# Causal attention scores: split products with mask matmuls, replaced by plain fp32 products with the mask on VectorE

## The chip, the core and the metric

The kernel runs on one core of a Trainium2 chip. The metric is the device time of one execution in microseconds (us). The core's engines work side by side, each through a queue of its own that it takes in order: TensorE (PE, with its weight loads as PEld), VectorE (DVE), ScalarE (ACT), GpSimd (POOL) and SyncE (SP), which issues the DMA transfers. They wait for one another by semaphores.

## The reference

Two batches of 448 tokens go through causal attention with 12 heads of 64 channels, then a token mixer and channel mixer, then a Fourier mixer and a second channel mixer. The change touches the attention scores alone:

```python
scale = 1.0 / np.sqrt(q.shape[-1])                     # 1/8
scores = scale * np.matmul(q, k.transpose(0, 1, 3, 2))
mask = np.triu(np.ones((seq, seq), dtype=bool), k=1)
scores = np.where(mask, -1000000000.0, scores)
scores = scores - np.max(scores, axis=-1, keepdims=True)
attn = np.exp(scores)
attn = attn / (np.sum(attn, axis=-1, keepdims=True) + 1e-09)
return np.matmul(attn, v).astype(np.float32)
```

All inputs and outputs are fp32 or, for the weights, fp64 that the kernel converts.

## The kernel before

**The twelve pairs.** Attention runs over 12 pairs of heads (n = 0 to 11, six for each batch). A pair's q and k lie with their 64 channels on partitions 0 to 63 for the first head (e = 0) and 64 to 127 for the second. The 448 query rows are cut into four blocks of 112 (i = 0 to 3); block i needs only the first 112 x (i + 1) keys. A pair passes through these steps, named by one letter each:

- K: DMA of k and q, issued by SP (`load_k`). Before, the targets are idle tiles of the residual (`stage`): a ring of six and, from pair 5 on, of three.
- k, l, q, m (pairs 3 to 11): k and q are split into a high part in fp32r (ACT: `k_high`, and `q_high`, which also scales by 1/8) and a low remainder (POOL: `k_low`; DVE: `q_low`). e (pairs 0 to 2): DVE scales q in place, in two halves.
- S: scores on PE, in groups g. Pair 0 has four groups, one block each; the others three, of which g = 0 holds blocks 0 and 1. Each group takes two neighbouring banks of PSUM, one for each head (`grab` with n=2). Pairs 0 to 2 use plain fp32 matmuls, which PE runs as two passes; pairs 3 to 11 use three fp32r matmuls, high x high, high x low and low x high. Behind them come four bf16 matmuls for a group, which add -1e9 above the diagonal (`maskb`, with `identb` as weights).
- N: DVE takes the negated maximum of a block, both heads in one reduction. E: ACT takes the exponential from PSUM, one instruction for each head, with the negated maximum as bias and the row sum as a second output. The banks are given back after E.
- T: transposes of the exponentials on PE; C: copies of them out of PSUM on DVE and ACT; P: the product with v on PE; O: its copy on ACT; X: transposes back; Z and x: the division by the sums on DVE; h and g: the split of the result on ACT and POOL.

**What sets the order.** The table `ORDER` (line 73) lists these steps, and those of the token mixer that follow each half batch (A, B, D and their copies r, s, b, d, u, w) and of the first weights' conversion (R, W), as one sequence. Every engine takes its own instructions in exactly that sequence. PSUM has eight banks; a step that needs one takes the bank that was given back longest ago, with a preference of pairs for the lower four. Behind the table come the matmuls of the two channel mixers, over weights that ACT and DVE convert from fp64 a few tiles ahead.

**Lines.** The scores are line 366, the mask matmuls 380, the reduction 388, the exponential 398; q scaling 338, q low 342, k low 329, k high 325, q high 334; transposes 412, their copies 421, the product with v 430, the divisors 443 and 444, the division 463.

Of the kernel before, what the change touches and what calls it, by code (L numbers as in the profile page):

```python
# [72 lines left out]
ORDER = """K0 e0.0 S0.1 S0.0 e0.1 K1 S0.2 e1.0 N0.1 K2 N0.0 S0.3 E0.1 N0.2 S1.0 e2.1 E0.0 e1.1 S1.1 N0.3 V0 K3 N1.1 E0.2  # L73
e2.0 N1.0 E0.3 S1.2 T0.2 N1.2 E1.1 V1 C0.2 K4 N1.3 T0.4 T0.0 E1.0 R0 T0.1 T0.3 E1.2 C0.0 S2.1 C0.1 C0.4 S2.0
C0.3 S2.2 E1.3 q3 k3 P0 N2.2 Z0 N2.0 l3 T1.1 N2.1 E2.2 E2.1 O0 m3 T1.2 Z1 T1.0 T1.4 E2.0 N2.3 C1.2 C1.0 E2.3
C1.4 V3 k4 X0 T1.3 x0 S3.0 S3.1 C1.1 l4 Z2 N3.1 q4 S3.2 W0.0 C1.3 N3.0 K5 P1 E3.0 N3.2 T2.0 m4 E3.2 O1 E3.1 T2.2
W0.1 C2.0 T2.1 T2.3 X1 T2.4 B0.0 C2.1 C2.2 N3.3 C2.3 k5 S4.1 b0.0 x1 S4.2 h0 C2.4 E3.3 V2 N4.2 S4.0 P2 T3.2 E4.2
T3.4 N4.3 N4.1 T3.0 l5 W0.2 N4.0 E4.3 R1 g0 K6 W0.3 q5 O2 V5 T3.3 E4.1 X2 T3.1 C3.0 E4.0 C3.4 m5 x2 T4.2 k6 C3.1
T4.0 S5.1 C3.3 C3.2 h2 N5.2 l6 P3 W0.4 E5.2 S5.0 O3 N5.0 C4.0 C4.2 S5.2 g2 B0.2 h1 T4.4 W1.0 T4.3 W0.5 N5.1 N5.3
b0.2 T4.1 C4.1 g1 K7 A0.0 B0.1 C4.4 W1.1 q6 A0.1 R2 q7 V4 m7 C4.3 Z4 E5.0 E5.3 W1.2 E5.1 m6 Z3 r0.0 b0.1 X3 r0.1  # L80
P4 S6.0 O4 S6.1 W1.3 s0.0 W1.4 x3 T5.3 Z5 T5.2 N6.1 T5.1 s0.1 k7 N6.0 C5.3 W1.5 T5.4 C5.2 T5.0 E6.0 C5.1 l7 E6.1
X4 N6.2 C5.0 D0.1 K8 x4 V6 S6.2 E6.2 R3 S7.0 C5.4 W2.0 N6.3 k8 N7.1 S7.1 h4 P5 E6.3 N7.2 V7 D0.0 B1.1 E7.2 q8
T6.4 l8 K9 d0.1 E7.1 O5 T6.0 W2.1 b1.1 g4 X5 m8 T6.2 D0.2 N7.0 C6.0 C6.4 E7.0 x5 d0.0 W3.0 T6.3 T6.1 h5 C6.3
d0.2 C6.2 S7.2 S8.0 S8.1 g5 N7.3 C6.1 h3 N8.0 N8.2 S8.2 k9 N8.1 E7.3 N8.3 g3 P6 T7.3 Z7 E8.2 l9 E8.3 W3.1 q9
T7.0 W2.2 B1.0 C7.3 K10 q10 u0.2 C7.0 W2.3 T7.2 A1.1 Z6 W3.2 T7.4 T7.1 O6 E8.1 A1.0 b1.0 W2.4 B1.2 C7.1 m10 C7.2
C7.4 X6 k10 r1.0 m9 P7 r1.1 s1.0 S9.2 E8.0 b1.2 S9.0 R4 s1.1 O7 x6 S9.1 u0.0 N9.3 h6 T8.4 X7 N9.2 E9.3 N9.1 V8
D1.0 E9.2 x7 V9 C8.4 T8.3 T8.0 T8.2 d1.0 C8.2 N9.0 l10 C8.0 W3.3 K11 g6 T8.1 u1.0 C8.1 w0.2 C8.3 q11 S10.0 u0.1
w1.0 S10.2 E9.1 N10.1 N10.3 P8 k11 N10.0 E9.0 T9.4 T9.2 W3.4 D1.1 m11 Z8 C9.2 O8 E10.3 T9.0 V11 w0.0 E10.1 T9.3
E10.0 l11 D1.2 X8 h7 T9.1 C9.3 d1.1 C9.4 C9.0 d1.2 S11.2 S11.0 W2.5 x8 u1.1 h8 S10.1 N11.3 C9.1 S11.1 N11.0
E11.3 g7 N10.2 E10.2 P9 T10.1 N11.2 T10.0 N11.1 T10.3 E11.0 V10 E11.1 E11.2 C10.3 C10.0 g8 T10.2 Z9 T10.4 w1.1  # L90
C10.4 R5 Z10 A2.0 C10.2 C10.1 P10 W3.5 T11.4 w0.1 O9 T11.2 W4.0 W4.1 T11.0 T11.1 C11.4 O10 u1.2 W5.0 T11.3 W4.2
C11.3 C11.0 C11.1 A2.1 r2.0 C11.2 P11 X9 B2.1 X10 w1.2 W5.1 W4.3 B2.0 r2.1 B2.2 s2.0 s2.1 b2.1 D2.0 x9 R6 W4.4
x10 W5.2 D2.1 W5.3 O11 W4.5 W5.4 Z11 U2 y2 h10 X11 h9 D2.2 z2 b2.0 d2.1 R7 g10 W5.5 x11 d2.0 U0 W6.0 h11 W6.1
B3.0 g11 b3.0 g9 U3 A3.0 y0 y3 A3.1 r3.0 B3.2 b3.2 W6.2 z0 r3.1 s3.0 W7.0 W6.3 s3.1 U1 u2.0 W6.4 D3.1 b2.2 B3.1
D3.0 b3.1 y1 W7.1 W7.2 D3.2 W7.3 u2.1 W6.5 w2.0 W7.4 z1 z3 W7.5 d3.1 d2.2 d3.0 u3.1 w3.1 d3.2 Y0 u2.2 Y1 u3.2
w2.1 u3.0 a0 w3.0 w2.2 a1 w3.2
# [8 lines left out]
def fused_kernel(ctx: ExitStack, tc: tile.TileContext, qk, v, w1, w2, wa, wb, wc, wd, fa, fb, out):  # L105
# [100 lines left out]
    def grab(key, uses=1, n=1):  # L206
        old = {b: i + FAR * ((b < 4) == (n == 2)) for i, b in enumerate(ring)}
        if n == 2:
            old = {b: max(old[b], old[b + 1]) for b in range(0, 8, 2) if b in old and b + 1 in old}
        b = min(old, key=old.get)  # L210
        k = list(range(b, b + n))
        for b in k:
            ring.remove(b)
# [62 lines left out]
    with ExitStack() as actx:  # L276
# [3 lines left out]
        identb = a1.tile([128, 2, TS], BF16, name="identb")  # L280
        maskb = a1.tile([128, 2, 2, TS], BF16, name="maskb")
        vec.memset(identb, 0.0)
        vec.memset(maskb, 0.0)
        for e in range(2):
            for hb in range(2):
                he = slice(D * e, D * e + TS // 2)
                pool.affine_select(
                    out=identb[he, hb], in_=identb[he, hb], pattern=[[-1, TS]], compare_op=ALU.not_equal, fill=1.0,
                    base=hb * TS // 2, channel_multiplier=1,
                )  # L290
                pool.affine_select(
                    out=maskb[he, hb], in_=maskb[he, hb], pattern=[[0, 2], [-1, TS]], compare_op=ALU.is_ge, fill=-1.0e9,
                    base=hb * TS // 2, channel_multiplier=1,
                )
# [9 lines left out]
        staged = [0]  # L304

        def stage(n):
            staged[0] += 1
            return resid[staged[0] % 6 if n < 5 else 3 + staged[0] % 3][1]

        def load_k(n):  # L310
            c = pairs[n]
            b, hp = n // 6, n % 6
# [4 lines left out]
            parts = (slice(0, 2 * TS), slice(2 * TS, S)) if n == 0 else (slice(0, S),)
            for cols in parts:
                for t, part in todo:
                    nc.sync.dma_start(out=t[:, cols], in_=qk[b, hp, :, part, cols])  # L320

        def k_high(n):
            c = pairs[n]
            c.kh, c.kl = [kq.tile([128, S], F32R, tag=t, name=t) for t in ("kh", "kl")]
            act.copy(c.kh, c.k32)

        def k_low(n):
            c = pairs[n]
            (pool if n else vec).tensor_tensor(out=c.kl, in0=c.k32, in1=f(c.kh), op=ALU.subtract)

        def q_high(n):
            c = pairs[n]
            c.qh, c.ql = [kq.tile([128, S], F32R, tag=t, name=t) for t in ("qh", "ql")]
            act.activation(out=c.qh, in_=c.q32, func=AF.Copy, scale=0.125)

        def q_scale(n, part):
            cols = pairs[n].q32[:, 2 * TS * part : 2 * TS * (part + 1)]
            vec.tensor_scalar(out=cols, in0=cols, scalar1=0.125, scalar2=None, op0=ALU.mult)

        def q_low(n):  # L340
            c = pairs[n]
            vec.scalar_tensor_tensor(out=c.ql, in0=c.q32, scalar=0.125, in1=f(c.qh), op0=ALU.mult, op1=ALU.subtract)
# [9 lines left out]

        def scores(n, g):
            c = pairs[n]
            if not hasattr(c, "sp"):
                c.sp, c.se = {}, {}
            sp = c.sp[g] = grab(("S", n, g), 1 if g or not n else 2, 2)
            se = c.se[g] = [sp[:TS, e] for e in range(2)]
            blocks = BLOCKS[g] if n else BLOCKS_0[g]
            for i, c0 in blocks:  # L360
                w = TS * (i + 1) if n < PLAIN else max(256, TS * (i + 1))
                passes = ((c.q32, c.k32),) if n < PLAIN else ((c.qh, c.kh), (c.qh, c.kl), (c.ql, c.kh))
                for m, (qt, kt) in enumerate(passes):
                    for e in range(2):
                        he = slice(D * e, D * e + D)
                        mm(  # L366
                            se[e][:, c0 : c0 + w], lhsT=qt[he, i * TS : (i + 1) * TS], rhs=kt[he, :w],
                            start=m == 0 and (i != 1 or n == 0), stop=False, skip_group_check=True,
                        )
# [674 lines left out]
```

## Time and profile before

| | before |
|---|---|
| median of 3 runs | 682.4 us (682.19 to 682.69) |
| profiled execution, its own time | 681.78 us |
| its span, first to last instruction | 679.9 us |
| PE busy | 674.3 us (99%) |
| DVE busy | 540.2 us (79%) |
| ACT busy | 288.3 us (42%) |
| POOL busy | 124.4 us (18%) |
| PE's share of the chain of work that ended last | 98% |
| granted TensorE clock | 1.000 |

Busy time is the share of the span in which an engine had an instruction under way. The ends of matmuls are modelled, so a full PE row says that PE always had something in it, and not that it went at its peak. An instruction that waits inside the engine, behind another engine's hold of a port, counts as busy. The clock of 1.000 is the higher of TensorE's two levels, 2.4 GHz. The pairs' work lies in the first 102 us or so; the profile's rows for DVE, ACT and POOL are full there and thin out later.

### The profile page before, as it was taken

How to read it: one execution, taken by the hardware profiler on the slowest of the kernel's cores; microseconds unless marked ns; L12 is line 12 of the kernel's file. 1: busy time of each engine (PE TensorE's matmuls, PEld its weight loads, DVE VectorE, ACT ScalarE, POOL GpSimd, SP SyncE). 2: the span in 40 equal slices, each digit the busy share in tenths (PEclk: the TensorE clock that was granted, in tenths of full speed). 3: DMA queues.
4: the chain of work that ended last, by engine and by line, in shares of the span. 5: the costliest groups of instructions: out<-in, count | busy, mean ns of one | idle time of the engine just before them, and what ended most of it. 6: DMA issues, size and time to landing. Idle time of an engine off the chain costs nothing.

```text
span 679.9 us, 10227 instructions
## 1 busy us (share of the span) xinstructions
PE 674.3 (99%) x3922; PEld 618.5 (91%) x3922; DVE 540.2 (79%) x888; ACT 288.3 (42%) x619; POOL 124.4 (18%) x102
## 2 busy tenths in 40 slices
PE   8999999999999999999999999999999999999997
PEld 6888888999999999999999999999999999999997
DVE  6988896597987965799989868989877899646851
ACT  6989894444243332235555522313423333323200
POOL 2235272330000000220330006281002320000000
PEclk9999999999999999999999999999999999999999
DMA  7433311174443332200223332323332533222311
GB/s 213 146 110 130 115 38 70 57 244 143 152 146 117 127 107 93 94 1 1 93 94 104 132 137 94 115 90 136 125 103 83 184 113 138 94 92 76 113 44 55
DMA packets 20865, 73.38 MB, mean 108 GB/s; under 512 B 2366, under 2 KB 7230, under 8 KB 20448
## 3 DMA queue, kind: packets, MB, share of 16 engines
...
q14 instruction: 18, 0.15, 0.1%
...
## 4 chain that ended last, share of the span: by engine, by line
PE 98%; DMA 0%; DVE 0%; SPq 0%; issue 0%; ACT 0%; DVEq 0%
PE psum L242 13%; PE psum L262 13%; PE psum L266 13%; PE psum L267 13%; PE psum L243 13%; PE psum L241 13%; PE psum L430 4%; PE psum L412 4%; PE psum L366 3%; PE psum L499 3%; PE psum L533 2%; PE psum L735 2%; PE psum L804 1%; PE psum L450 1%; PE psum L519 1%; PE psum L380 1%
## 5 line engine op out<-in xcount | busy, mean ns | idle before, releaser
L262 PE MATMUL psum<-gh,wh 128*128 128x448 f32 x432 | 157.5, 365 | 0.0
L242 PE MATMUL psum<-acth,wl 128*128 128x448 f32 x432 | 156.7, 363 | 0.0
L267 PE MATMUL psum<-gl,wh 128*128 128x448 f32 x432 | 156.6, 362 | 0.0
L266 PE MATMUL psum<-gh,wl 128*128 128x448 f32 x432 | 156.6, 362 | 0.0
L241 PE MATMUL psum<-acth,wh 128*128 128x448 f32 x432 | 156.6, 362 | 0.0
L243 PE MATMUL psum<-actl,wh 128*128 128x448 f32 x432 | 156.0, 361 | 0.0
L143 ACT ACTIVATE m<-w 128x512 f32<-128x512 f32 (+2 forms) x92 | 71.1, 774 | 120.2 <-DVE wl L163 83.1
L161 ACT CAST wh<-m 128x512 fp32r<-128x512 f32 (+1 forms) x90 | 63.5, 705 | 94.8 <-PE psum L267 55.5
L241 PEld LDWEIGHTS psum<-acth,wh 128*128 128x128 f32 x432 | 81.0, 188 | 6.1
L267 PEld LDWEIGHTS psum<-gl,wh 128*128 128x128 f32 x432 | 81.0, 188 | 5.9
L262 PEld LDWEIGHTS psum<-gh,wh 128*128 128x128 f32 x432 | 81.1, 188 | 5.7 <-issue 0.2
L266 PEld LDWEIGHTS psum<-gh,wl 128*128 128x128 f32 x432 | 81.0, 188 | 5.7 <-issue 0.2
L242 PEld LDWEIGHTS psum<-acth,wl 128*128 128x128 f32 x432 | 81.1, 188 | 4.9
L243 PEld LDWEIGHTS psum<-actl,wh 128*128 128x128 f32 x432 | 80.9, 187 | 5.2
L150 DVE SCALAR_TENSOR_TENSOR m<-w,m 128x512 uint32<-128x512 uint32 (+2 forms) x92 | 80.3, 873 | 2.3
L163 DVE TENSOR_TENSOR wl<-m,wh 128x512 fp32r<-128x512 f32 (+1 forms) x84 | 69.5, 830 | 14.6 <-ACT wh L161 14.1
L154 DVE SCALAR_TENSOR_TENSOR m<-w,m 128x512 uint32<-128x512 uint32 (+2 forms) x92 | 79.2, 861 | 2.0
L145 DVE TENSOR_SCALAR m<-m 128x512 f32<-128x512 f32 (+2 forms) x92 | 51.2, 557 | 32.1 <-ACT m L143 32.0
L247 ACT ACTIVATE gh<-psum 128x448 fp32r<-128x448 f32 x72 | 37.8, 541 | 69.5 <-PE psum L243 69.3
L249 DVE SCALAR_TENSOR_TENSOR gl<-psum,gh 128x448 fp32r<-128x448 f32 x72 | 43.7, 619 | 29.7 <-ACT gh L247 29.7
L146 DVE TENSOR_SCALAR m<-m 128x512 uint32<-128x512 uint32 (+2 forms) x92 | 49.0, 532 | 2.4
L398 ACT ACTIVATE p<-psum,nmx 112x224 f32<-112x224 f32 (+3 forms) x96 | 46.7, 520 | 6.1 <-DVE nmx L388 5.8
...
## 6 DMA issues: line engine op xcount, KB each, us to landing
...
```

Of the source, the lines that this page charges most:

```text
L143: act.activation(out=m, in_=hi.bitcast(F32), func=AF.Abs)
L145: vec.tensor_scalar(out=m, in0=m, scalar1=F64_MIN, scalar2=F64_MAX, op0=ALU.max, op1=ALU.min)
L150: vec.scalar_tensor_tensor(out=mu, in0=lo, scalar=29, in1=mu, op0=ALU.logical_shift_right, op1=ALU.bitwise_or)
L154: vec.scalar_tensor_tensor(out=mu, in0=hi, scalar=0xC0000000, in1=mu, op0=ALU.bitwise_and, op1=ALU.bitwise_or)
L161: act.copy(wh, m)
L163: low_engine[0].tensor_tensor(out=wl, in0=m, in1=f(wh), op=ALU.subtract)
L241: mm(pb[:, :S], lhsT=lh, rhs=act_h[ct][b], start=ct == 0, stop=False)
L242: mm(pb[:, :S], lhsT=ll, rhs=act_h[ct][b], start=False, stop=False)
L243: tail[0] = mm(pb[:, :S], lhsT=lh, rhs=act_l[ct][b], start=False, stop=ct == NCT - 1).ins
L262: mm(pb[:, :S], lhsT=lh, rhs=gh, start=j + k == 0 and seeded is None, stop=False, skip_group_check=seeded is not None,)
L266: mm(pb[:, :S], lhsT=ll, rhs=gh, start=False, stop=False, skip_group_check=seeded is not None)
L267: tail[0] = mm(pb[:, :S], lhsT=lh, rhs=gl, start=False, stop=j == last and k == nk - 1, skip_group_check=seeded is not None,).ins
```

## The change

Scores of all pairs are plain fp32 products of unsplit, unscaled q and k, as those of pairs 0 to 2 were. There are no mask matmuls and no parts of q and k; the steps k, l, q, m and e are gone from `ORDER`, and the other words of it stay in their order. One fp32 tile `mask` (0, and -8e9 above the diagonal of its last 112 columns) is made at the start by a memset on DVE and one select on POOL, where before there were two memsets and eight selects.

N is now, for each head of a block, one custom instruction of DVE, `tensor_tensor_reduce`. It adds the scores in PSUM and the mask in SBUF, multiplies by -1/8, writes the result to `p` in SBUF and gives its minimum as `nmx`. E reads `p` in SBUF, with a scale of -1, and writes it in place. A group takes one bank for each head, and a bank is given back after N. q and k have tiles of their own (the tags that held the parts before), two buffers for even and two for odd pairs.

```diff
-    def grab(key, uses=1, n=1):
-        old = {b: i + FAR * ((b < 4) == (n == 2)) for i, b in enumerate(ring)}
...
+    def grab(key, uses=1):
+        k = [ring.pop(0)]
         held[key] = k, [uses]
...
+        mask = a1.tile([TS, S], F32, name="mask")
+        vec.memset(mask, 0.0)
+        pool.affine_select(
+            out=mask[:, S - TS :], in_=mask[:, S - TS :], pattern=[[-1, TS]], compare_op=ALU.is_ge, fill=MASKED,
+            base=0, channel_multiplier=1,
+        )
...
-            c.k32, c.q32 = stage(n), stage(n)
+            c.k32, c.q32 = [kq.tile([128, S], F32, tag=t + "hl"[n % 2], name=t + "32") for t in "kq"]
...
-                passes = ((c.q32, c.k32),) if n < PLAIN else ((c.qh, c.kh), (c.qh, c.kl), (c.ql, c.kh))
...
+            for i, c0 in blocks:
                 for e in range(2):
+                    he = slice(D * e, D * e + D)
+                    mm(
+                        c.sc[i, e][0], lhsT=c.q32[he, i * TS : (i + 1) * TS], rhs=c.k32[he, : TS * (i + 1)],
+                        start=c0 == 0, stop=True, skip_group_check=True,
+                    )
...
-                    mm(dst, lhsT=identb[he, hb], rhs=rhs, start=False, stop=hb == 1, skip_group_check=True)
...
-            vec.tensor_reduce(out=c.nmx[:, i], in_=c.sp[g][:TS, :, c0 : c0 + w], axis=AX.X, op=ALU.max, negate=True)
...
+                sc, bank_of = c.sc[i, e]
+                vec.tensor_tensor_reduce(
+                    out=c.p[:, e, OFF[i] : OFF[i] + w], in0=sc, in1=mask[:, S - w :], scale=-SCALE, scalar=3.0e38,
+                    op0=ALU.add, op1=ALU.min, accum_out=c.nmx[:, i, e],
+                )
+                drop(bank_of)
...
-                    out=c.p[:, e, OFF[i] : OFF[i] + w], in_=c.se[g][e][:, c0 : c0 + w], func=AF.Exp,
-                    bias=c.nmx[:, i, e], scale=1.0, accum_out=c.ssum[:, i, e],
                 )
-            drop(("S", n, g))
+                    out=p, in_=p, func=AF.Exp, bias=c.nmx[:, i, e], scale=-1.0, accum_out=c.ssum[:, i, e],
```

The next two pieces are DVE's queue at the start of the program, from the last memset on: before, then after. `resid_1_78`, `resid_1_82` and `resid_1_74` hold q of pairs 0, 1 and 2 there.

```order
L204 MEMSET eps_t 128x1
L338 TENSOR_SCALAR resid_1_78<-resid_1_78 128x224 x2
L338 TENSOR_SCALAR resid_1_82<-resid_1_82 128x224
L388 TENSOR_REDUCE nmx<-psum 112x2 x3
L338 TENSOR_SCALAR resid_1_74<-resid_1_74 128x224
L338 TENSOR_SCALAR resid_1_82<-resid_1_82 128x224
```

```order
L202 MEMSET eps_t 128x1
L327 ISA p,nmx<-psum,mask 112x224
L327 ISA nmx 112x1
L327 ISA p,nmx<-psum,mask 112x224
L327 ISA nmx 112x1
```

The scalings of q ahead of the first reduction are gone, that of pair 1 among them. Each reduction has become two custom instructions (the rows `ISA p,nmx`), each with one that writes a single column behind it.

The next two pieces are PE's queue at the scores of pair 3: before, the last group (block 3) from the last mask matmul of the group ahead of it to the first of its own four; after, the whole pair and the product with v behind it. `kh`, `kl`, `qh`, `ql` are the high and low parts; `k_193` and `q_194` are the tiles of pair 3.

```order
L380 LDWEIGHTS identb
L380 MATMUL psum<-maskb,identb 112x112
L366 MATMUL psum<-kh,qh 112x448 x2
L366 MATMUL psum<-kl,qh 112x448 x2
L366 MATMUL psum<-kh,ql 112x448 x2
L380 LDWEIGHTS identb
L380 MATMUL psum<-maskb,identb 112x112
```

```order
L314 MATMUL psum<-k_193,q_194 112x112 x2
L314 MATMUL psum<-k_193,q_194 112x224 x2
L314 MATMUL psum<-k_193,q_194 112x336 x2
L314 MATMUL psum<-k_193,q_194 112x448 x2
L369 MATMUL psum<-pt,v 64x448 x2
```

The three fp32r products of a group, and its four mask matmuls with weight loads of their own (one is shown), have become one plain product for each head, which PE runs in two passes.

## Rows read from the trace of the kernel before

**Rows 1.** Busy us (instructions) of PE, PEld, DVE, ACT, POOL in two stretches; clock, DMA.

```profile
11.10:34.00 22.90, 22.50 (x233) 18.10 (x232) 22.25 (x37) 22.73 (x76) 4.97 (x4) 1.00 0.52 166
34.00:102.00 68.00, 68.00 (x644) 57.00 (x643) 57.72 (x103) 59.82 (x181) 32.18 (x24) 1.00 0.30 98
```

**Rows 2.** ACT's waits over the span: for whom, us in total, times, longest.

```profile
ACT wh L161 <- PE psum L267: 55.5, 23, 4.8
```

**Rows 3.** Timeline of PE: start, us, line, shape (pairs 0, 2 and 3).

```profile
3.58 1.09 PE L366 MATMUL psum<-resid,resid 64*112 64x224 f32 x4 [0.32 <-DMA resid<-in_qk]
...
13.14 0.91 PE L366 MATMUL psum<-resid,resid 64*112 64x336 f32 x4
13.80 0.31 PE L380 MATMUL psum<-maskb,identb 56*112 56x112 bf16 x3
...
14.00 0.78 PE L366 MATMUL psum<-resid,resid 64*112 64x112 f32 x7
14.52 0.35 PE L380 MATMUL psum<-maskb,identb 56*112 56x224 bf16 x3
14.72 0.54 PE L366 MATMUL psum<-resid,resid 64*112 64x448 f32 x1
...
15.47 0.36 PE L380 MATMUL psum<-maskb,identb 56*112 56x112 bf16 x4
15.76 2.11 PE L430 MATMUL psum<-pt,v 112*64 112x448 f32 x16
...
20.30 0.38 PE L366 MATMUL psum<-kh,qh 64*112 64x256 f32 x2
...
22.71 2.11 PE L430 MATMUL psum<-pt,v 112*64 112x448 f32 x16
```

**Rows 4.** Reductions (line 388) in two stretches: length, DVE busy (count), clock, DMA.

```profile
11.10:34.00 22.90, 9.34 (x13) 1.00 0.52 166
34.00:102.00 68.00, 19.57 (x28) 1.00 0.30 98
```

**Rows 5.** Groups of DVE by shape: count, busy us, mean ns, idle before (0 to 102).

```profile
L388 DVE TENSOR_REDUCE nmx<-psum 112x2 f32<-112x896 f32 x12 | 13.0, 1081 | 2.8 <-PE psum L380 2.8
...
L388 DVE TENSOR_REDUCE nmx<-psum 112x2 f32<-112x224 f32 x12 | 4.6, 380 | 2.8 <-PE psum L380 2.3 <-ACT pt L421 0.3 <-ACT p L398 0.2
```

**Rows 6.** Timeline of DVE: start, us, line, shape, idle before and its releaser.

```profile
5.85 0.28 DVE L338 TENSOR_SCALAR resid<-resid 128x224 f32<-128x224 f32 x1 [1.79 <-DMA resid<-in_qk]
6.05 1.68 DVE L388 TENSOR_REDUCE nmx<-psum 112x2 f32<-112x448 f32 x3
...
14.97 0.16 DVE L443 SCALAR_TENSOR_TENSOR ssum<-ssum 112x8 f32<-112x8 f32 x1
...
16.07 0.62 DVE L342 SCALAR_TENSOR_TENSOR ql<-resid,qh 128x448 fp32r<-128x448 f32 x1
16.60 1.12 DVE L443 SCALAR_TENSOR_TENSOR ssum<-ssum 112x8 f32<-112x8 f32 x1
...
21.08 1.08 DVE L443 SCALAR_TENSOR_TENSOR ssum<-ssum 112x8 f32<-112x8 f32 x1
```

**Rows 7.** Timeline of ACT: a copy, an exponential, its read of the sum, the next.

```profile
13.41 0.63 ACT L421 COPY pt<-psum 112x448 f32<-112x448 f32 x1
13.83 0.74 ACT L398 ACTIVATE p<-psum,nmx 112x448 f32<-112x448 f32 x1
14.36 0.31 ACT L398 ACTIVATION_READ_ACCUMULATOR p<-psum,nmx 112x1 f32 x1
14.45 0.74 ACT L398 ACTIVATE p<-psum,nmx 112x448 f32<-112x448 f32 x1
```

**Rows 8.** The q low parts (line 342), columns as in rows 4.

```profile
11.10:34.00 22.90, 1.23 (x2) 1.00 0.52 166
34.00:102.00 68.00, 4.89 (x7) 1.00 0.30 98
```

**Rows 9.** Timeline of POOL: a k low part.

```profile
16.33 1.36 POOL L329 TENSOR_TENSOR kl<-resid,kh 128x448 fp32r<-128x448 f32 x1 [12.63 <-ACT kh L325]
```

More of the change, by code (lines that the diff above doesn't have):

```diff
@@ L38 @@
 EARLY_DOWN = (0, 3)
-PLAIN = 3
-FAR = 4
+SCALE = 0.125
+MASKED = -1.0e9 / SCALE
 ORDER2 = """
@@ L92 @@
[L92 to L96, printed above, removed]
+ORDER = """K0 S0.1 S0.0 K1 S0.2 N0.1 K2 N0.0 S0.3 E0.1 N0.2 S1.0 E0.0 S1.1 N0.3 V0 K3 N1.1 E0.2 N1.0 E0.3 S1.2 T0.2 N1.2
@@ new lines @@
+B0.2 h1 T4.4 W1.0 T4.3 W0.5 N5.1 N5.3 b0.2 T4.1 C4.1 g1 K7 A0.0 B0.1 C4.4 W1.1 A0.1 R2 V4 C4.3 Z4 E5.0 E5.3 W1.2
+E5.1 Z3 r0.0 b0.1 X3 r0.1 P4 S6.0 O4 S6.1 W1.3 s0.0 W1.4 x3 T5.3 Z5 T5.2 N6.1 T5.1 s0.1 N6.0 C5.3 W1.5 T5.4 C5.2
+T5.0 E6.0 C5.1 E6.1 X4 N6.2 C5.0 D0.1 K8 x4 V6 S6.2 E6.2 R3 S7.0 C5.4 W2.0 N6.3 N7.1 S7.1 h4 P5 E6.3 N7.2 V7
+D0.0 B1.1 E7.2 T6.4 K9 d0.1 E7.1 O5 T6.0 W2.1 b1.1 g4 X5 T6.2 D0.2 N7.0 C6.0 C6.4 E7.0 x5 d0.0 W3.0 T6.3 T6.1 h5
+C6.3 d0.2 C6.2 S7.2 S8.0 S8.1 g5 N7.3 C6.1 h3 N8.0 N8.2 S8.2 N8.1 E7.3 N8.3 g3 P6 T7.3 Z7 E8.2 E8.3 W3.1 T7.0
@@ new lines @@
+N11.1 T10.3 E11.0 V10 E11.1 E11.2 C10.3 C10.0 g8 T10.2 Z9 T10.4 w1.1 C10.4 R5 Z10 A2.0 C10.2 C10.1 P10 W3.5
+T11.4 w0.1 O9 T11.2 W4.0 W4.1 T11.0 T11.1 C11.4 O10 u1.2 W5.0 T11.3 W4.2 C11.3 C11.0 C11.1 A2.1 r2.0 C11.2 P11
+X9 B2.1 X10 w1.2 W5.1 W4.3 B2.0 r2.1 B2.2 s2.0 s2.1 b2.1 D2.0 x9 R6 W4.4 x10 W5.2 D2.1 W5.3 O11 W4.5 W5.4 Z11 U2
+y2 h10 X11 h9 D2.2 z2 b2.0 d2.1 R7 g10 W5.5 x11 d2.0 U0 W6.0 h11 W6.1 B3.0 g11 b3.0 g9 U3 A3.0 y0 y3 A3.1 r3.0
+B3.2 b3.2 W6.2 z0 r3.1 s3.0 W7.0 W6.3 s3.1 U1 u2.0 W6.4 D3.1 b2.2 B3.1 D3.0 b3.1 y1 W7.1 W7.2 D3.2 W7.3 u2.1
@@ L97 @@
+W6.5 w2.0 W7.4 z1 z3 W7.5 d3.1 d2.2 d3.0 u3.1 w3.1 d3.2 Y0 u2.2 Y1 u3.2 w2.1 u3.0 a0 w3.0 w2.2 a1 w3.2
 """
@@ L204, in fused_kernel @@
     vec.memset(eps_t, EPS)
-    def grab(key, uses=1, n=1):
-        old = {b: i + FAR * ((b < 4) == (n == 2)) for i, b in enumerate(ring)}
[L208 to L213, printed above, removed]
+    def grab(key, uses=1):
+        k = [ring.pop(0)]
         held[key] = k, [uses]
-        return psum[:, k[0]] if n == 1 else psum[:, k[0] : k[0] + 2]
+        return psum[:, k[0]]
     def drop(key):
@@ L278, in fused_kernel @@
         a1 = actx.enter_context(tc.tile_pool(name="attn1", bufs=1))
[L280 to L294, printed above, removed]
+        mask = a1.tile([TS, S], F32, name="mask")
[4 more added lines that the diff above has]
+        )
         make_identity(nc, ident)
@@ L303, in fused_kernel @@
         halves = [Pair() for _ in range(2 * B)]
[L304 to L308, printed above, removed]
         def load_k(n):
             c = pairs[n]
-            b, hp = n // 6, n % 6
-            c.k32, c.q32 = stage(n), stage(n)
-            todo = (c.k32, 1), (c.q32, 0)
-            if n < PLAIN:
-                todo = todo[::-1]
+            c.k32, c.q32 = [kq.tile([128, S], F32, tag=t + "hl"[n % 2], name=t + "32") for t in "kq"]
             parts = (slice(0, 2 * TS), slice(2 * TS, S)) if n == 0 else (slice(0, S),)
             for cols in parts:
[L319 to L342, printed above, removed]
+                for t, part in ((c.q32, 0), (c.k32, 1)):
+                    nc.sync.dma_start(out=t[:, cols], in_=qk[n // 6, n % 6, :, part, cols])
         def load_v(n):
@@ L346, in load_v @@
             nc.sync.dma_start(out=pairs[n].v, in_=v[n // 6, n % 6])
-        BLOCKS = ((0, 256), (1, 0)), ((2, 0),), ((3, 0),)
-        HOME = (0, 256), (0, 0), (1, 0), (2, 0)
+        BLOCKS = ((0, 0), (1, 256)), ((2, 0),), ((3, 0),)
         BLOCKS_0 = tuple(((i, 0),) for i in range(NI))
-        HOME_0 = tuple((i, 0) for i in range(NI))
         def scores(n, g):
             c = pairs[n]
[L355 to L358, printed above, removed]
+            if not hasattr(c, "sc"):
+                c.sc = {}
@@ L359, in scores @@
             blocks = BLOCKS[g] if n else BLOCKS_0[g]
+            for e in range(2):
+                sb = grab(("S", n, g, e), len(blocks))
+                for i, c0 in blocks:
+                    c.sc[i, e] = sb[:TS, c0 : c0 + TS * (i + 1)], ("S", n, g, e)
             for i, c0 in blocks:
-                w = TS * (i + 1) if n < PLAIN else max(256, TS * (i + 1))
-                passes = ((c.q32, c.k32),) if n < PLAIN else ((c.qh, c.kh), (c.qh, c.kl), (c.ql, c.kh))
[L363 to L369, printed above, removed]
@@ L385, in maxima @@
                 c.nmx = small(ap, "nmx")
-            g, c0 = HOME[i] if n else HOME_0[i]
+                c.p = ap.tile([TS, 2, 1120], F32, tag="p", name="p")
             w = TS * (i + 1)
-            vec.tensor_reduce(out=c.nmx[:, i], in_=c.sp[g][:TS, :, c0 : c0 + w], axis=AX.X, op=ALU.max, negate=True)
+            for e in range(2):
+                sc, bank_of = c.sc[i, e]
[4 more added lines that the diff above has]
+                drop(bank_of)
         def exps(n, i):
             c = pairs[n]
-            if not hasattr(c, "p"):
+            if not hasattr(c, "ssum"):
                 c.ssum = small(tiny, "ssum")
-                c.p = ap.tile([TS, 2, 1120], F32, tag="p", name="p")
-            g, c0 = HOME[i] if n else HOME_0[i]
-            w = TS * (i + 1)
             for e in range(2):
+                p = c.p[:, e, OFF[i] : OFF[i] + TS * (i + 1)]
                 act.activation(
-                    out=c.p[:, e, OFF[i] : OFF[i] + w], in_=c.se[g][e][:, c0 : c0 + w], func=AF.Exp,
-                    bias=c.nmx[:, i, e], scale=1.0, accum_out=c.ssum[:, i, e],
+                    out=p, in_=p, func=AF.Exp, bias=c.nmx[:, i, e], scale=-1.0, accum_out=c.ssum[:, i, e],
                 )
-            drop(("S", n, g))
         def transposes(n, u):
@@ L581, in fused_kernel @@
         ops = dict(
-            K=load_k, k=k_high, l=k_low, q=q_high, m=q_low, e=q_scale, V=load_v, S=scores, N=maxima, E=exps, T=transposes,
+            K=load_k, V=load_v, S=scores, N=maxima, E=exps, T=transposes,
             C=pt_copy, P=pv, O=pv_copy, Z=divisors, X=rows, x=divide, h=x_high, g=x_low, A=mix_in, r=mix_high,
```

38 lines of the change are left out of this document (10 added, 28 removed).

## The prediction

> **What bounds the kernel now.** I read the busy table first, then the timelines of PE, DVE, ACT and POOL over the first 102 us, where all twelve head pairs lie, and last the waits. In the stretch from 34 to 102 us PE is busy for all of its 68.00 us, with DVE at 57.72 and ACT at 59.82; from 11.1 to 34 us PE shows 22.50 of 22.90, but DVE 22.25 and ACT 22.73 [rows 1]. So the reader should see two regimes: an early one in which three engines are full at once and nobody has room, and a later one in which PE sets the pace and DVE has 10.3 us of slack in 68. After 102 us the change touches nothing; there ACT waits 55.5 us for PE to give its weight buffers back [rows 2], so PE paces the conversions, and a shift at 102 us should reach the end whole.
>
> **PE: what goes.** A plain pair before the change takes 15.76 - 13.14 = 2.62 us from its first score matmul to the next stage. Of that the mask matmuls hold PE from 13.80 to 14.00, 14.52 to 14.72 and 15.47 to 15.76, 0.69 us; the plain fp32 products alone take 0.66 + 0.52 + 0.75 = 1.93 us. A split pair with its masks takes 22.71 - 20.30 = 2.41 us [rows 3]. Afterwards every pair is plain and unmasked. Nine pairs gain 2.41 - 1.93 = 0.48 us, 4.3 in all, and three gain about 0.69, 2.1 in all: 6.4 us. For the last stretch, which holds the seven pairs 5 to 11, that is 7 x 0.48 = 3.4 us, so PE needs 64.6 us there.
>
> **DVE: what comes and goes.** A pair has four score blocks; 13 and 28 of the 48 lie in the two later stretches [rows 4], 7 before. Each reduction over both heads becomes two custom instructions, one for each head, and each of these brings a second instruction that reads the accumulator (the order shows both). The elements stay the same: the reduction takes 380 ns for 2 x 112 columns and 1081 ns for 2 x 448 [rows 5], 1.04 ns a column. A STT over 448 columns starts the next instruction 16.60 - 16.07 = 0.53 us later [rows 6], so 0.07 of it belongs to the instruction and not to its columns. Splitting a block therefore costs some 0.08 us more.
>
> The accumulator read is not in the trace on DVE. Below, it cannot cost less than an instruction without columns, 0.07 us. Above, ACT does the same thing with its sums: an exponential of 448 columns plus its read holds ACT from 13.83 to 14.45, 0.62 us (0.53 and 0.09), where a plain copy of 448 columns holds it 0.42 [rows 7]; so 0.20 with the pause before the read. I take 0.10 us, since the row nearest to it is the read's own 0.09, and DVE's part beside the columns is small. The Trainium skill, Vector Engine (DVE) Microarchitecture Reference, section Measured stream behaviour on trn2, states about 75 ns for each instruction beside its columns; by that the 96 reads would come to 7.2 us and not 9.6, and the forecast would fall by about one us.
>
> What leaves DVE: 2 and 7 of the nine q low parts in the second and third stretch [rows 8] at 0.53 us, and the six scalings of q at the start. With POOL's nine k low parts goes a hidden stall: the 112x8 divisor step takes 0.16 us at 14.97 but 1.12 at 16.60, while POOL's k low runs from 16.33 to 17.69 [rows 6, 9]. A second divisor step, at 21.08, takes 1.08 us. So 0.9 us goes twice in the second stretch; for the third I count none.
>
> **The sum, stretch by stretch.** Start, to 11.1 us: the first reduction starts at 6.05, because the scaling of pair 1's q stands ahead of it in DVE's queue and waits until 5.85 for its DMA, while its own scores end at 3.58 + 1.09 = 4.67 [rows 3, 6]. That wait goes: 1.4 us earlier. Three more scalings between the first reductions go too, at 6.05 - 5.85 = 0.20 us each. Seven blocks pay 7 x 0.08 + 14 x 0.10 = 2.0. Net 2.0 - 1.4 - 0.6 = 0. The exponentials also start earlier and PE no longer waits for them to give two banks back, but DVE still sets the end of this stretch.
>
> Second stretch, 13 blocks: 13 x 0.08 + 26 x 0.10 = 3.6 us in, 2 x 0.53 + 1.9 = 3.0 us out, and 0.65 us of DVE idle can take the rest: 0. PE's gain is lost here, since DVE is full; PE waits instead. ACT, full too, loses its passes over q and k, each no shorter than the copy's 0.42 us [rows 7]; that covers its exponentials, which now read SBUF, a price that the trace doesn't show, bounded by nothing and 0.1 us each, the size of ACT's other small steps.
>
> Third stretch, 28 blocks: 28 x 0.08 + 56 x 0.10 = 7.8 us in, 7 x 0.53 = 3.7 us out: DVE needs 57.7 + 4.1 = 61.8 us, PE 64.6. PE still sets the pace: -3.4. But DVE's idle shrinks from 10.3 to 2.8 us, and not every wait of an in-order queue can be squeezed; I take back 1.0 us (an estimate, about one wait in three of what stays). Total 0 + 0 - 3.4 + 1.0 = -2.4 us.
>
> The profiled execution took 681.78 us, 0.6 under the median of 682.4; 681.8 - 2.4 = 679.4 there, 680.0 against the median.
>
> **What costs nothing.** Loads: SP issues the same number in the same places. Their targets are now q and k tiles of their own, four pairs deep, where before a ring of six and then three tiles was shared; no load can wait longer. POOL swaps eight small selects for one ahead of the first score. PSUM banks come back after the new DVE instruction, not after the exponential, so sooner. The mask on DVE hangs only on that one select. If one of these covers failed, it would be in the first 10 us, for about a us.
>
> **Rivals.** 1. The read costs what it costs on ACT, 0.20. Then the first two stretches pay 40 x 0.10 = 4.0 us more, and in the third DVE needs 67.4 us, more than PE; with 1.0 for waits it is 68.4. Sum 4.0 + 0.4 = +4.4: 686.2 profiled, 686.8 by the median. It turns slower at about 0.155, where the 40 early reads eat the 2.4. For it: ACT's rows, the only reads in the trace, and the full second stretch. Against it: DVE's small instructions are shorter than ACT's. Chance 0.21.
>
> 2. The gain is given back in waits: the chain scores, minimum, exponential, transpose, copy goes through DVE three times a pair, and at 96% of PE's pace each late copy holds PE. If the third stretch keeps most of its idle, DVE ends where it did: 0, 682.4. Chance 0.17.
>
> 3. The read costs the bare 0.07 and no wait is left: -1.2 - 3.4 = -4.6, 677.8 by the median. Chance 0.15.
>
> 4. The custom instruction streams at half rate. One block of 448 columns would cost 0.47 us more, a pair 2240 x 1.04 ns = 2.3 us: five pairs in the full stretches 11.6, and in the third 61.8 + 7 x 2.3 + 1.0 = 78.9 against 68. Sum about +22, 705. Against it: the q low step reads two fp32 tensors from SBUF at one column a ns [rows 6], and the new instruction reads but one from SBUF; what it adds is the accumulator. The Trainium skill, Vector Engine (DVE) Microarchitecture Reference, section Points that are easy to get wrong, says that the instruction shape with two wide SBUF sources runs at half throughput, with no port left for the accumulator; the q low row does not show it, though without an accumulator. Chance 0.05.
>
> 5. The change doesn't do what it says on PE: unmasked plain products expose their weight loads, and a pair stays near 2.4. Then the third stretch gains nothing and DVE's cost early decides: about +0.5 to +1.5, 683.5. Chance 0.04.
>
> **How the numbers follow.** My forecast, a read of 0.08 to 0.13 us with about 1 us of waits, has 0.38: 680.0, itself from 678.5 to 681. A comparison of this kernel can tell some 0.2% (1.4 us) from no change. Faster: 0.38 + 0.15 = 0.53. Same: rival 2 and part of 5, 0.19. Slower: rivals 1 and 4 and the rest of 5, 0.28. The range takes in rivals 2 and 3 and rival 1 up to its far end, and leaves rival 4 and what lies beyond the bounds: 677 to 687.
>
> **What would show it.** The first DVE minimum should start near 4.7 us and not 6.05. The DVE timeline gives the read's price as the gap from one custom instruction to the next, less its columns and 0.07. A pair's scores on PE should take 1.9 to 2.0 us. From 11 to 34 us PE should wait for DVE, on transposes and on the copies ahead of PV; from 34 to 102 us hardly. POOL loses its 1.2 us steps, and the divisor steps shrink to 0.16 where no other POOL step runs. I am wrong if DVE is full to 102 us (the read above 0.15, rival 1), if PE's waits after 34 us exceed 2 us, or if a custom instruction of 448 columns takes near 1 us.

## The result, and the profile after

The changed kernel takes 675.75 us, median of 4 runs (675.71 to 677.15), beside 682.36 for the kernel before: a ratio of 0.9908, 95% interval 0.989 to 0.9925. It is faster by 6.6 us, where 2.4 were forecast, and 1.25 us below the low end of the range. The profiled execution took 675.74 us, its span is 673.6 (679.9 before).

Busy us (instructions) of PE, PEld, DVE, ACT and POOL in three stretches of the changed kernel, with clock and DMA; the last two answer to [rows 1]:

```profile
0.00:11.10 11.10, 10.22 (x64) 7.83 (x66) 6.83 (x36) 7.58 (x27) 0.98 (x7) 1.00 0.81 216
11.10:34.00 22.90, 22.90 (x188) 16.00 (x186) 21.92 (x77) 22.20 (x72) 1.54 (x2) 1.00 0.68 203
34.00:102.00 68.00, 68.00 (x528) 52.48 (x525) 55.66 (x181) 57.43 (x167) 25.59 (x19) 1.00 0.27 93
```

PE is now full in both later stretches. Where the time went is read from one mark that every pair has, the start of its product with v (16 matmuls of line 430, now 369). Timeline of PE in the changed kernel, start, us, line and shape:

```profile
8.69 2.13 PE L351 MATMUL psum<-ident,p 112*112 112x112 f32 x20
...
13.40 2.11 PE L369 MATMUL psum<-pt,v 112*64 112x448 f32 x16
...
17.94 2.15 PE L314 MATMUL psum<-k,q 64*112 64x112 f32 x16
20.02 2.11 PE L369 MATMUL psum<-pt,v 112*64 112x448 f32 x16
...
24.94 2.15 PE L314 MATMUL psum<-k,q 64*112 64x336 f32 x16
27.02 2.11 PE L369 MATMUL psum<-pt,v 112*64 112x448 f32 x16
...
33.22 2.11 PE L369 MATMUL psum<-pt,v 112*64 112x448 f32 x16
...
103.86 2.11 PE L369 MATMUL psum<-pt,v 112*64 112x448 f32 x16
```

The same marks in the kernel before, beside 15.76 and 22.71 of [rows 3]:

```profile
10.47 0.98 PE L412 MATMUL psum<-ident,p 112*112 112x112 f32 x8
...
27.76 0.41 PE L366 MATMUL psum<-kh,qh 64*112 64x336 f32 x2
...
30.38 2.11 PE L430 MATMUL psum<-pt,v 112*64 112x448 f32 x16
...
36.52 2.11 PE L430 MATMUL psum<-pt,v 112*64 112x448 f32 x16
...
110.12 2.11 PE L430 MATMUL psum<-pt,v 112*64 112x448 f32 x16
```

The first mark comes 15.76 - 13.40 = 2.36 us earlier, the fourth 36.52 - 33.22 = 3.30, the last 110.12 - 103.86 = 6.26. So the start gave 2.36 us, the second stretch 0.94, the third 2.96. The spans differ by 6.3: what stands at the last mark reaches the end whole.

The price on which the forecast turned stands in DVE's timeline after the change:

```profile
10.39 0.61 DVE L327 CUSTOM_DVE_ANT_0 p<-psum,mask 112x448 f32<-112x448 f32 x1
10.93 0.08 DVE L327 DVE_READ_ACCUMULATOR2_ANT nmx<- 112x1 f32 x1
10.93 0.62 DVE L327 CUSTOM_DVE_ANT_0 p<-psum,mask 112x448 f32<-112x448 f32 x1
11.47 0.08 DVE L327 DVE_READ_ACCUMULATOR2_ANT nmx<- 112x1 f32 x1
11.47 1.15 DVE L360 COPY pt<-psum 112x448 f32<-112x448 f32 x2
12.54 0.50 DVE L327 CUSTOM_DVE_ANT_0 p<-psum,mask 112x336 f32<-112x336 f32 x1
```

A read shows 0.08 us, but it starts where the instruction ahead of it stops holding the engine, and the next instruction starts at the same time. From custom instruction to custom instruction are 10.93 - 10.39 = 0.54 us, and the two copies hold DVE for 12.54 - 11.47 = 1.07. So a start-to-start time shows next to nothing for the read, and the custom instruction streams as fast as a copy.

### The profile page after: what moved, and what is told of

It is laid out like the page before. It is cut to its first block, busy times and chain, and to the rows that moved or that the text cites. A ratio compares the mean times of both kernels' runs of the same rounds, so it can differ in the third digit from the quotient of the medians.

```text
span 673.6 us, 9830 instructions
## 1 busy us (share of the span) xinstructions
PE 669.0 (99%) x3702; PEld 607.1 (90%) x3702; DVE 535.0 (79%) x1016; ACT 282.4 (42%) x601; POOL 111.2 (17%) x86
## 4 chain that ended last, share of the span: by engine, by line
PE 99%; DVE 0%; issue 0%
PE psum L254 13%; PE psum L234 13%; PE psum L258 13%; PE psum L259 13%; PE psum L233 13%; PE psum L235 13%; PE psum L314 4%; PE psum L369 4%; PE psum L351 4%; PE psum L438 3%; PE psum L472 2%; PE psum L674 2%; PE psum L743 1%; PE psum L389 1%; PE psum L458 1%; PE psum L195 0%
## 5 line engine op out<-in xcount | busy, mean ns | idle before, releaser
L339 ACT ACTIVATE p<-p,nmx 112x224 f32<-112x224 f32 (+3 forms) x96 | 49.6, 521 | 3.9 <-DVE nmx L327 3.8
```

## Experiments

Each run is compared with runs of the kernel before on the same chip; times below are the ratio by 682.4 us, so the changed kernel is 676.1. The theory: the forecast's sum held, and only the price of the read was wrong. Put 0 in place of 0.10 for the 40 early reads, and 680.0 becomes 676.0 (676.6 if the 0.65 us of DVE idle that the forecast filled in the second stretch stay idle). The rival: PE paces the early stretches too, DVE's price hardly matters, and the agreement is chance.

**The price of the read: noread, pay10, pay09, pay15, pay20.** noread takes the accumulator output away; the row minimum is left out.

```diff
-    op0=ALU.add, op1=ALU.min, accum_out=c.nmx[:, i, e],
+    op0=ALU.add, op1=ALU.min, accum_out=None,
...
-    out=p, in_=p, func=AF.Exp, bias=c.nmx[:, i, e], scale=-1.0, ...
+    out=p, in_=p, func=AF.Exp, bias=zero[:TS], scale=-1.0, ...
```

> The changed kernel without the accumulator output of the new DVE instruction, so without the 96 reads behind it; the exponentials take a bias of zero, so the row minimum is left out of the computation. Theory (the read costs DVE nothing from start to start, since in the changed kernel the next instruction starts 0.54 us after a 448-column one, read included): the same time as the changed kernel, 675.0 to 676.5 us, with the DVE instructions at the same pace. Rival 1 (the read does hold DVE for some 0.05 to 0.08 us, and the columns run faster than a copy's): 40 early reads come off, 2 to 3 us, so 673 to 674. Rival 2 (the sum was wrong elsewhere and the reads matter through the exponentials that wait for them): up to 1 us faster.

Measured: 0.9904 (0.989 to 0.9918), 675.9 us. Without its 96 reads the kernel is as fast as with them. Timeline of DVE, noread:

```profile
10.56 1.15 DVE L327 CUSTOM_DVE_ANT_0 p<-psum,mask 112x448 f32<-112x448 f32 x2
11.62 1.15 DVE L360 COPY pt<-psum 112x448 f32<-112x448 f32 x2
```

Two custom instructions hold DVE for 11.62 - 10.56 = 1.06 us here, and for 11.47 - 10.39 = 1.08 with their reads. So a read costs about 0.01 us.

The other four give the read a price again, by small memsets behind each custom instruction; pay10 has one, pay15 two, pay20 three, pay09 one and two in turn (shown):

```diff
+    pad = a1.tile([TS, 16], F32, name="pad")
...
     vec.tensor_tensor_reduce(... accum_out=c.nmx[:, i, e])
+    for _ in range(1 + e):
+        vec.memset(pad, 0.0)
```

> The changed kernel with one small DVE memset (16 columns of a scratch tile) behind each new DVE instruction: 96 of them, each expected to hold DVE for 0.06 to 0.10 us, which is about the price that the prediction gave to the accumulator read. Theory A (only this price was wrong, the rest of the prediction's sum holds): the two early stretches, with 40 of them, lose 40 x 0.06 to 0.10 = 2.4 to 4.0 us against 675.75, the later one nothing: 678.2 to 679.8, near the prediction's 680.0. Theory B (PE sets the pace in the early stretches as well, and DVE has room there): under 1 us lost, 675.7 to 676.7.

> The changed kernel with three small DVE memsets (16 columns each) behind each new DVE instruction: 288 of them, 0.18 to 0.30 us for each block and head. Theory A (the prediction's sum with only the read's price wrong): 40 x 0.18 to 0.30 = 7 to 12 us in the early stretches, and in the later one DVE passes PE: 55.7 + 56 x 0.18 to 0.30 = 65.8 to 72.5 us against PE's 68, so a further 0 to 5 us: 683 to 692. Theory B (PE sets the pace early too, with 3 to 5 us of room on DVE): 678 to 682.

> The changed kernel with small DVE memsets (16 columns of a scratch tile) behind the new DVE instructions: one behind the first head's, two behind the second head's. In pay10 one memset hid beside the read and moved the next instruction by 0.02 us; in pay20 each further one moved it by 0.135. So a block pays 0.02 + 0.155 us, 0.09 for each instruction: nearly the 0.10 that the prediction gave to the read. Theory A (only that price was wrong, the sum around it holds): the 40 early ones cost 40 x 0.09 = 3.6 us and the later ones nothing: 679.0 to 680.0, where 680.0 was predicted. Theory B (PE sets the pace in the early stretches too and has room for it): under 1.3 us lost, 676 to 677.5.

> As pay09, with two memsets behind each new DVE instruction: 0.155 us each by the steps of pay20, the price at which the prediction's first rival said that the change stops paying. Theory A: 40 x 0.155 = 6.2 us in the early stretches; in the later one DVE needs 55.7 + 56 x 0.155 = 64.4 us of 68, so nothing there, or one us for waits: 682 to 683.5, the same as the kernel before. Theory B (PE's pace hides a part of it): 678 to 680.

The price that they set is read from DVE's timeline, here in pay15:

```profile
16.25 0.25 DVE L328 CUSTOM_DVE_ANT_0 p<-psum,mask 112x112 f32<-112x112 f32 x1
16.26 0.07 DVE L333 MEMSET pad<- 112x16 f32 x1
16.42 0.08 DVE L328 DVE_READ_ACCUMULATOR2_ANT nmx<- 112x1 f32 x1
16.46 0.07 DVE L333 MEMSET pad<- 112x16 f32 x1
16.59 0.37 DVE L328 CUSTOM_DVE_ANT_0 p<-psum,mask 112x224 f32<-112x224 f32 x1
```

The next custom instruction starts 0.34 us later, where it is 0.195 without memsets: two cost some 0.15. The memset next to a custom instruction hides beside it (16.25 and 16.26), so pay10, meant as 0.06 to 0.10, set only about 0.02.

| run | price added, us | the forecast's sum with that price, us | measured: ratio (interval), us |
|---|---|---|---|
| the changed kernel | 0 | 676.0 | 0.9908 (0.989 to 0.9925), 676.1 |
| pay10 | 0.02 | 676.8 | 0.991 (0.9895 to 0.9924), 676.3 |
| pay09 | 0.09 | 679.6 | 0.9948 (0.9935 to 0.9962), 678.9 |
| pay15 | 0.155 | 682.2 | 1.0011 (0.9997 to 1.0026), 683.2 |
| pay20 | 0.29 | 691.5 to 692.5 | 1.0151 (1.013 to 1.0172), 692.7 |

The third column is 676.0 + 40 x price; for pay20 DVE's need in the third stretch comes on top, 55.7 + 56 x 0.29 = 71.9 us against 68, and up to 1 us of waits. The totals follow it along the whole line, at 0.155 too, where the first rival put the turn. The rival, with 676 to 677.5 at 0.09 and 678 to 680 at 0.155, is out. Whether the price is paid where the sum has it is looked at below, in pay_late.

Some executions lose time to the granted clock as well. In four of pay15's twelve its mean is 0.994 or 0.995, and they take 684.9 to 685.5 us; the other eight take 681.7 to 682.9, which by the ratio is 682.1. Two windows of pay20 (columns as above):

```profile
34.00:44.00 10.00, 7.73 (x54) 4.84 (x52) 8.95 (x48) 6.55 (x20) 0.00 (x0) 0.93 0.32 96
44.00:50.00 6.00, 6.00 (x29) 3.05 (x28) 1.36 (x12) 3.83 (x9) 4.18 (x3) 0.54 0.30 113
```

PE was busy for 7.73 of 10 us, and then the granted clock stood at 0.54, near the lower of its two levels, 1.2 GHz; a product with v takes 4.00 us there and not 2.11. This execution took 695.4 us, the longest of pay20's four. But the one whose mean clock was 1.00 took 692.5, so the agreement doesn't hang on the clock.

**Early or late: pay_late.** pay15's loop with `range(2 * (n >= 5))`, so that the third stretch alone pays.

> As pay15 (two small memsets, 0.155 us, behind each new DVE instruction), but only for pairs 5 to 11, whose 56 instructions lie behind 34 us: 8.7 us of DVE time. Theory (the prediction's split of the program: DVE sets the end early, PE late): DVE's 12 us of idle there take it, 0 to 1.6 us lost, 675.7 to 677.4. Rival (an in-order queue can't use its idle time; the price counts everywhere): more than 3 us lost, 679 or above.

Measured: 0.9933 (0.9921 to 0.9945), 677.8 us. Timeline of PE in pay_late, then in pay15:

```profile
34.63 2.11 PE L372 MATMUL psum<-pt,v 112*64 112x448 f32 x16
...
106.87 2.11 PE L372 MATMUL psum<-pt,v 112*64 112x448 f32 x16
```

```profile
15.01 2.11 PE L372 MATMUL psum<-pt,v 112*64 112x448 f32 x16
...
37.90 2.11 PE L372 MATMUL psum<-pt,v 112*64 112x448 f32 x16
...
110.14 2.11 PE L372 MATMUL psum<-pt,v 112*64 112x448 f32 x16
```

From the fourth mark to the last are 72.24 us in both, 70.64 in the changed kernel: 8.7 us of new DVE work cost 1.60, at the upper end of the theory. In pay15's trace the second stretch, from the first mark to the fourth, takes 37.90 - 15.01 = 22.89 us, and 33.22 - 13.40 = 19.82 in the changed kernel. That is 3.07 more, where 26 prices are 4.0; in pay09 it is 1.26 (35.06 - 13.98 = 21.08) where they are 2.3. The missing us fits the 22.90 - 21.92 = 0.98 that DVE had free there. With 1.61 at the start, pay15's trace pays 4.7 us of the early 6.2, and 1.6 late, where the sum has nothing. So its total agrees in part by luck. By the ratios, with pay15's eight executions at full clock, it is 682.1 - 677.8 = 4.3 us early, and 677.8 - 676.1 = 1.7 for the late 8.7. DVE's price counts for most of its size early and for a fifth late: the prediction's split of the program, but not as sharp.

**The start: scale_back, before_start, two_queues.** scale_back puts the six scalings back into the changed kernel:

```diff
-ORDER = """K0 S0.1 S0.0 K1 S0.2 N0.1 ...
+ORDER = """K0 e0.0 S0.1 S0.0 e0.1 K1 S0.2 e1.0 N0.1 ...
+    vec.tensor_scalar(out=cols, in0=cols, scalar1=1.0, scalar2=None, op0=ALU.mult)
```

> The changed kernel with the six scalings of q put back where they stood in the kernel before, here as multiplications by 1.0 on DVE, so that the first minimum again stands behind a step that waits for pair 1's q. Theory (the start's shift is carried whole to the end): the first minimum starts at about 6.05 instead of 4.58, and the time rises by 1.4 to 2.4 us, to 677.2 to 678.2. Rival (the start is bound by something else, the first loads or the exponentials): under 0.5 us.

Measured: 0.9926 (0.9913 to 0.994), 677.4 us, 1.2 more. Timeline of DVE, scale_back:

```profile
5.98 0.28 DVE L298 TENSOR_SCALAR q<-q 128x224 f32<-128x224 f32 x1 [1.67 <-DMA q<-in_qk]
6.17 0.39 DVE L332 CUSTOM_DVE_ANT_0 p<-psum,mask 112x224 f32<-112x224 f32 x1
```

The first minimum starts at 6.17 instead of 4.58, and all twelve marks stand 1.6 us later in this trace (14.99 to 105.47). So the wait and the scalings, 2.0 us in the prediction's sum, cost 1.6 in the changed kernel's trace and 1.2 by the ratios, whose intervals overlap. before_start takes the wait out of the kernel before:

```diff
-... K1 S0.2 e1.0 N0.1 K2 N0.0 S0.3 ...
+... K1 S0.2 N0.1 K2 N0.0 e1.0 S0.3 ...
```

> The kernel before with one word of the order moved: the scaling of pair 1's q stands behind pair 0's first two reductions instead of ahead of them. Theory (DVE's wait sets the start, and a shift there is carried to the end): the first reduction starts near 4.7 us instead of 6.05 and the time falls by 0.8 to 1.5 us, 681 to 681.6. Rival (PE with its mask matmuls sets the start, or pair 1's scores wait for the scaling just as long): less than 0.4 us.

Measured: 0.9999 (0.999 to 1.0008), nothing. Timeline of DVE, then of PE, before_start:

```profile
4.72 1.04 DVE L388 TENSOR_REDUCE nmx<-psum 112x2 f32<-112x448 f32 x2 [0.67 <-PE psum L380]
```

```profile
8.54 0.82 PE L366 MATMUL psum<-resid,resid 64*112 64x336 f32 x4 [0.49 <-ACT p L398]
...
10.29 1.12 PE L412 MATMUL psum<-ident,p 112*112 112x112 f32 x8
```

The first reduction starts at 4.72, 1.3 us earlier, as expected; but the first transposes at 10.29 instead of 10.47. PE, with its mask matmuls and a wait for ACT to give banks back, ends this stretch as late as DVE did; DVE loses its lead too, as its next scalings wait 0.71 us for their own q at 7.93. The rival stands: something else held the start as long, and taking the wait away pays only where that is gone too. With the wait left in and the masks gone, scale_back's first mark is 15.76 - 14.99 = 0.77 us ahead of the kernel before. Whether that is the masks or the earlier return of the banks was not separated.

two_queues looks for more there: the k loads of pairs 0 and 1 go out on ACT's queue, ahead of its table load.

```diff
-nc.sync.dma_start(out=t[:, cols], ...)
+(nc.scalar if part and n < 2 else nc.sync).dma_start(out=t[:, cols], ...)
```

> The changed kernel with the k loads of pairs 0 and 1 issued from ACT's queue instead of SP's, ahead of the table load, so that the first four loads are issued in about half of the 1.9 us that SP takes for them. Theory (a shift of the start is carried whole to the end, as scale_back showed): the first score products start 0.3 to 0.6 us earlier and the time falls by as much, 675.1 to 675.5. Rival (the transfers themselves, not their issue, set the start, or ACT's first exponential comes later): no change or up to 0.5 us slower.

Measured: 0.9914 (0.99 to 0.9927), 676.5 us: no gain. Timeline of ACT's queue and of PE:

```profile
0.73 1.37 ACTq L291 DMA_DIRECT2D k<-in_qk  x3
```

```profile
3.40 5.89 PE L315 MATMUL psum<-k,q 64*112 64x224 f32 x32 [0.15 <-DMA k<-in_qk]
```

The three k loads are issued by 2.10 us, yet PE starts at 3.40 (3.36 without the change). So the issue of the loads doesn't set PE's start. That the transfers do fits a DMA share of 0.81 in the first stretch (above), but is not shown. The transposes start at 9.22 instead of 8.69, as this trace has more of the slow first products that the last section tells of.

**The two halves: split_mask_dve, plain_mask_pe, plain_mask_own.** split_mask_dve has the new DVE instruction, no mask matmuls, and split products for pairs 3 to 11:

```diff
-passes = ((c.q32, c.k32),)
+passes = ((c.q32, c.k32),) if n < 3 else ((c.qh, c.kh), (c.qh, c.kl), (c.ql, c.kh))
```

> Half of the change: the mask, scale and minimum in the new DVE instruction, but pairs 3 to 11 keep their scores as three products of split q and k, without mask matmuls; the split of q and k on ACT, DVE and POOL is back, as are the shared staging tiles; q isn't scaled. It tells which half of the change PE's gain belongs to. Theory M (the mask matmuls carry it: a split pair without its masks takes about 2.41 - 0.39 = 2.02 us on PE, a plain one 2.08): PE's time stays, and only DVE's two early q low steps (1.1 us) and POOL's stall of the divisor steps (1.9 us) come back, part of them hidden: 675.5 to 678. Theory S (the plain products carry it, as the prediction's 1.93 us said): nine pairs lose 0.1 us more, and what DVE loses early comes in full: 678 to 680.

Measured: 0.998 (0.997 to 0.999), 681.0 us, more than both expected. Timeline of PE, pair 4, and a wait behind it:

```profile
27.43 0.41 PE L321 MATMUL psum<-kh,qh 64*112 64x336 f32 x2
...
29.38 2.11 PE L376 MATMUL psum<-pt,v 112*64 112x448 f32 x16
...
61.95 0.65 PE L396 MATMUL psum<-ident,ots 128*112 128x128 f32 x4 [1.80 <-ACT ots L384]
```

On PE theory M holds: 29.38 - 27.43 = 1.95 us a pair, against 2.08 for the plain pair at 24.94 to 27.02. So the loss isn't PE's own. The second stretch takes 21.81 us from first to fourth mark (19.82), which was not traced further, and one pair (from the sixth mark to the seventh) 13.59 instead of 10.24. There ACT's k high waits, in ACT's timeline:

```profile
56.56 0.56 ACT L283 CAST kh<-resid 128x448 fp32r<-128x448 f32 x1 [1.50 <-DMA resid<-in_qk]
```

Behind it in ACT's queue stand the exponentials and the copy ots for which PE then waits 1.80 us; from 64 to 66 us the granted clock is 0.50, its lower level. The load that it waits for goes into a shared staging tile, and the order is that of another kernel; which of the two is at fault wasn't tried.

The other half is the kernel before with `PLAIN = 12`, mask matmuls and reductions untouched, and `e` in place of `q`, `k`, `l`, `m` in the order. In plain_mask_pe the later loads wait for the shared staging tiles and overwrite them too soon, so that it is another computation:

> The other half: the kernel before with all twelve pairs plain, q scaled in place on DVE where it was split, but with mask matmuls, reductions over two heads and exponentials out of PSUM as before. Theory M: nine pairs go from 2.41 to 2.62 us on PE, 9 x 0.21 = 1.9 us slower, of which DVE's and POOL's relief in the early stretch gives back up to 1.0: 683 to 684.5. Theory S (plain products are as good as or better than split ones): 680.5 to 682.4.

It took 688.75 us (1.0091), with PE waiting for q; that says nothing on the question. With tiles of its own:

> plain_mask_pe again, with q and k tiles of their own for each pair as in the changed kernel, instead of the shared staging tiles, which its later loads waited for and overwrote: all pairs plain, mask matmuls, reductions and exponentials as in the kernel before. Theory M (the mask matmuls carry PE's gain, plain and split products cost PE about the same): 682 to 684, as before or up to 2 us slower. Theory S (plain products carry it): 679 to 681.

Measured: 1.0033 (1.0021 to 1.0046), 684.7 us. Timeline of PE, pair 3:

```profile
21.07 0.83 PE L342 MATMUL psum<-k,q 64*112 64x112 f32 x8
...
23.60 2.11 PE L406 MATMUL psum<-pt,v 112*64 112x448 f32 x16
```

Plain with masks takes 23.60 - 21.07 = 2.53 us, split with masks 2.41 [rows 3], plain without masks 2.08. So the masks are worth 0.45 us a pair, and plain products cost PE 0.12; split_mask_dve's 1.95 gives the same two within 0.01. In one pair, 11.77 us from mark to mark instead of 10.41, two scalings of q hold DVE up; timelines of DVE and of POOL:

```profile
72.14 0.46 DVE L314 TENSOR_SCALAR q<-q 128x224 f32<-128x224 f32 x2
...
89.19 3.03 DVE L314 TENSOR_SCALAR q<-q 128x224 f32<-128x224 f32 x2
```

```profile
87.31 2.95 POOL L523 TENSOR_TENSOR actl<-resid,acth 128x448 fp32r<-128x448 f32 x2 [2.35 <-ACT acth L519]
90.23 1.86 POOL L139 TENSOR_TENSOR wl<-m,wh 128x768 fp32r<-128x768 f32 x1
```

They take 0.46 us at 72.14, where POOL is idle, and 3.03 while POOL subtracts, the stall that the divisor steps of [rows 6, 9] showed. The Trainium skill, SBUF — State Buffer, section Who interferes with whom, says that the two engines share one pair of ports, which the instruction that comes first holds to its end, while the other engine's is blocked. These rows agree.

The halves give -1.4 and +2.3 us, the whole -6.3. So they don't add up: without masks PE waits, at the place shown, for ACT behind a part of the split, and without the split PE keeps the masks. Neither half has an order written for it, so how much of this is the order's stays open.

## Why the prediction was wrong

**The step that failed is the price of the accumulator read**, 0.10 us with 0.07 as its floor; the runs show about 0.01. The floor rested on "it cannot cost less than an instruction without columns". That holds for the read's busy time, 0.08, but not from start to start: the read lies under the end of the instruction ahead of it. The prediction took its value from ACT's read, where the next instruction does start later, 0.09 us [rows 7]. In the forecast's sum 40 early reads are 4.0 us of the 4.25 missed (3.4 with that idle time kept), and as a floor the price set the range's low end too. The runs give it a little less: 0.09 us added in pay09 cost 678.9 - 676.1 = 2.8 us, so 0.10 would cost about 3.1. The Trainium skill, Vector Engine (DVE) Microarchitecture Reference, section Measured stream behaviour on trn2, gives a built-in operation of one or two sources some 75 ns for each instruction, beside its columns. For this read the trace does not agree.

**The stretches.** With a free read the sum gives 1.4 for the start, 2.0 for the second stretch and 2.4 for the third, 5.8; measured 2.36, 0.94 and 2.96, 6.26. The total is right, its division less so. In the second stretch PE should have waited for DVE; it is busy for 22.90 of 22.90 us, DVE for 21.92, so with the read near nothing PE sets the pace here too, and the stretch gains what PE saves on pairs 3 and 4, 2.41 - 2.08 = 0.33 and (30.38 - 27.76) - 2.08 = 0.54. In the start the wait, the scalings and the masks left together, and "DVE still sets the end of this stretch" was half true: before_start shows PE as late as DVE. A start can also be up to 1.4 us slower than this one with the same work (below), so the 2.36 is that of one execution. That 5.8 comes so near to 6.26 is in part luck.

**PE.** An unmasked plain pair takes 2.08 us, 1.93 forecast: the row of the plain pair had its mask matmuls overlapping its products, so taking their stretches out took too much. The third stretch's 2.96 for seven pairs is 0.42 each, between the 0.33 and 0.54 of pairs 3 and 4. The forecast's 0.48 a pair was too much and the 1.0 us taken back for waits wasn't needed; the two errors partly cancel in its 2.4. That PE sets the pace there was right.

**DVE.** The first minimum starts at 4.58 (4.7 forecast). The divisor steps take 0.16 to 0.17 us at 13.39, 14.67 and 18.71, so POOL's stall is gone. Splitting a block costs the 0.08 that was forecast: two instructions of 448 columns take 11.47 - 10.39 = 1.08 us, the reduction over both heads 12.71 - 11.71 = 1.00 in the trace before.

**ACT.** Exponentials of 448 columns show the same busy time from SBUF as from PSUM, 661 and 659 ns, but here too the start-to-start time tells more. Timeline of ACT after the change:

```profile
13.41 0.65 ACT L339 ACTIVATE p<-p,nmx 112x448 f32<-112x448 f32 x1
...
14.06 0.56 ACT L339 ACTIVATE p<-p,nmx 112x336 f32<-112x336 f32 x1
```

One of 448 columns takes 14.06 - 13.41 = 0.65 us with its read, where it took 14.45 - 13.83 = 0.62 [rows 7]; 224 columns take 9.59 - 9.12 = 0.47, before 7.56 - 7.14 = 0.42. So the price is some 0.03 to 0.05 us, inside the forecast's bounds.

**Rivals.** 3 was nearest, the same mechanism at 0.07. 1's turning point agrees with pay15, its price is refuted. 2 is out: nothing was given back after the fourth mark. 4 is out: 448 columns take 0.54 us, not 1.0. The Trainium skill's rule that stands beside it, on two wide SBUF sources (Vector Engine (DVE) Microarchitecture Reference, section Points that are easy to get wrong), is tried by no run here with an accumulator, since the scores come from PSUM. 5 is out at 2.08.
